# A linear-attention and ReLU-gate block: key weight in five pieces, the query weight loaded late, queries of chunk 1 first, z column three blocks later

## The chip, the cores and the metric

The kernel runs on one core of a Trainium2 chip. The metric is the device time of one execution in microseconds (us); lower is better. Single executions of one kernel scatter here by about 0.3%, so differences of less than 0.7 us are read from the traces, and times are quoted as the median of all runs together with a ratio to the kernel before.

Engines are called as in the profile: PE is TensorE (matmul), DVE is VectorE, ACT is ScalarE, POOL is GpSimd, SP is SyncE, which here only issues DMAs.

## The reference, cut to what matters

```python
# x: 2048 x 640; H = 32 heads of 20; all bf16
xn = layernorm(x)                                   # no scale or bias
q, k, v = split(xn @ wqkv)                          # 3 x (2048 x 640)
phi = lambda t: where(t > 0, t + 1, exp(t)) + 1e-6
kv  = einsum("bhsd,bhse->bhde", phi(k), v)          # per head 20 x 20
z   = einsum("bhsd->bhd", phi(k))                   # sum of the keys over the sequence
o   = (phi(q) @ kv) / (phi(q) . z + 1e-6)
s   = o @ wo
g   = silu(relu(xn @ w1) @ w2)                      # inner size 1728
out = x + s * g
```

## The kernel before: the parts that matter

The 2048 rows are 16 tiles of 128, in 4 chunks of 4 tiles. Chunk 0 is treated apart: its tiles are centred, transposed on PE and multiplied before their variance is known; they are normalised and transposed only later, for the query blocks and the G blocks. From tile 4 on a tile is normalised on DVE (`LN_norm`) and transposed by a DMA (`xnT_dma`), issued by SP. For each chunk PE makes 13 H blocks (`x @ w1`, five matmuls of 512 columns, 1.08 us each), 5 query blocks of the same size, and in between a key product per tile (`K_mm`, ten matmuls of 320 columns, 1.36 us). Later come the G blocks (products of xn and phi(k)), then the products with w2 and the output.

The buffers that the argument needs (a psum bank is a buffer into which PE writes its results; a ring slot is one of a few buffers used in turn):

```python
def K_exp(t, b): ...   # ACT: exp of psum banks b, b+1 into ek[t % 4, 0]
def K_relu(t, b): ...  # ACT: relu of the same banks into ek[t % 4, 1]
def K_fin(t): ...      # DVE, two operations: pk[t] = min(exp, 1) + 1e-6 + relu, reads ek[t % 4]
                       #   so K_exp(4) must wait until K_fin(0) has read slot 0
# key products of tiles 4 and up all use psum banks 0 and 1,
#   so K_mm(5) must wait until K_exp(4) and K_relu(4) have read them
def LN_stats(t): ...   # DVE: two bn_stats, one bn_aggr; then POOL: 1 / sqrt(var + eps)
def LN_norm(t):
    ...                # DVE: xn[t] = (x[t] - mean) * rstd, waits for POOL
    if t + XR < T:
        x_load(t + XR) # SP: next x tile into the slot just read
def z_add(): ...       # POOL: zacc += pk[t], once for each of the 16 tiles
def z_split(): ...     # POOL: zacc as two bf16 parts
def z_col(): ...       # PE: turns these into a column, then DVE builds zmat
```

Load order at the start (SP issues in this order), and the loop over chunks, cut:

```python
x_load(0); x_load(1)
w_load(wqk[:, 0:KA, D:2 * D], ..., ("wk", 0))     # key weight, 2 of 5 row blocks
x_load(2)
w_load(wqk[:, KA:C, D:2 * D], ..., ("wk", 1))     # the other 3
x_load(3)
w1_load(0, "SP"); w1_load(1, "SP")
for t in range(4, XR):
    x_load(t)
...
    w1_load(2, "ACT")                             # 1040 KB, issued by ACT
    ...
    w_load(wqk[:, :, 0:D], A_wqkv[:, 0:D], ("wq",), E="ACT")   # 800 KB, right after it
...
qs = [[], [(0, f) ...] + [(1, f) ...], [(2, f) ...], [(3, f) ...]]   # query blocks by chunk of PE's order
...
            if j == 0:                            # chunk 0, after H block n
                if n in lnat[j]:                  # n = 0..3: tile 4..7
                    LN_stats(t)
                    if n >= 2:
                        K_fin(2 * n - 4); K_fin(2 * n - 3)     # beside the wait for POOL
                    LN_norm(t)
                    xnT_dma(t)
...
                if n == 6:                        # chunk 3
                    z_col()
```

## Time and profile before

| | before |
|---|---|
| median of 4 runs | 227.93 us (227.15 to 227.96) |
| profiled execution | 226.59 us, span of the core 224.9 us |
| PE busy | 215.8 us, 96% of the span |
| waits of PE that a schedule could remove | 4.2 us |

Whether PE is the limit is seen on the page of before, in the busy times and in the clock by slices of the span.

```profile
span 224.9 us, 3501 instructions
...
PE 215.8 (96%) x1432; PEld 132.9 (59%) x1442; DVE 114.9 (51%) x212; ACT 87.1 (39%) x143; POOL 46.7 (21%) x69
...
PEclk9999999999999999999999999999999999999999
```

PE is busy almost always, at the full clock. So the time can fall only where PE stands still. The waits of PE in before say where: engine, buffer and line that waited, what it waited for, then us in total, number of waits, longest.

```profile
PE psT L650 <- POOL regE L645: 1.4, 1, 1.4
PE psT L486 <- DMA reg<-reg: 1.2, 1, 1.2
PE psT L380 <- DVE zero L370: 1.0, 1, 1.0
PE psT L539 <- DMA reg<-reg: 0.6, 1, 0.6
PE psT L486 <- DVE mv L413: 0.4, 1, 0.4
PE psT L486 <- DMA reg<-in_A_wqkv_dram: 0.3, 1, 0.3
```

(The last two lines of that answer, 0.2 us each, are cut.) L650 is the z column, L486 the key products, L539 the query blocks; "reg<-reg" is a transposing DMA. The line L380 is the start of the program. The same waits stand in the timeline of PE of before (start in us, length in us, line, shapes, count, and in brackets the idle time ahead and its end):

```profile
13.03 6.42 PE L561 MATMUL psT<-regX,reg 128*128 128x512 bf16 x29
20.65 1.53 PE L486 MATMUL psT<-reg 128*128 128x320 bf16 x10 [1.20 <-DMA reg<-reg]
...
24.18 1.52 PE L486 MATMUL psT<-reg 128*128 128x320 bf16 x10
...
37.66 1.25 PE L539 MATMUL psT<-reg 128*128 128x512 bf16 x5 [0.61 <-DMA reg<-reg]
...
98.62 0.40 PE L650 MATMUL psT<-ones,regE 128*128 128x1 bf16 x10 [1.36 <-POOL regE L645]
...
114.33 21.90 PE L776 MATMUL psT<-reg 128*128 128x320 bf16 x160
```

13.03 is the first group of H blocks (one of 30 records is missing, so it really began near 12.8). 20.65 is the key product of tile 4, 24.18 that of tile 5, 37.66 the first query block, 98.62 the z column, 114.33 the G blocks. The end of a matmul is modelled. Blocks of five matmuls of 512 columns follow each other every 1.08 us, 0.216 us for each, but a block is shown as 1.24 us long. So an idle time in brackets is about 0.16 us too short.

On DVE, the timeline of before shows tile 4 normalised at 15.04, tile 5 at 17.52, and the first operation of K_fin(0) at 18.92, ahead of the normalisation of tile 6:

```profile
15.04 0.45 DVE L428 TENSOR_SCALAR reg<-reg,mv,rsy 128x640 bf16<-128x640 bf16 x1 [0.99 <-POOL rsy L417]
...
17.52 0.45 DVE L428 TENSOR_SCALAR reg<-reg,mv,rsy 128x640 bf16<-128x640 bf16 x1 [0.99 <-POOL rsy L417]
...
18.92 0.27 DVE L519 TENSOR_SCALAR regE<-regE 128x640 bf16<-128x640 bf16 x1
```

### The profile page before, as it was taken

How to read it: one execution, taken by the hardware profiler on the slowest of the kernel's cores; microseconds unless marked ns; L12 is line 12 of the kernel's file. 1: busy time of each engine (PE TensorE's matmuls, PEld its weight loads, DVE VectorE, ACT ScalarE, POOL GpSimd, SP SyncE). 2: the span in 40 equal slices, each digit the busy share in tenths (PEclk: the TensorE clock that was granted, in tenths of full speed). 3: DMA queues.
4: the chain of work that ended last, by engine and by line, in shares of the span. 5: the costliest groups of instructions: out<-in, count | busy, mean ns of one | idle time of the engine just before them, and what ended most of it. 6: DMA issues, size and time to landing. Idle time of an engine off the chain costs nothing.

```text
span 224.9 us, 3501 instructions
## 1 busy us (share of the span) xinstructions
PE 215.8 (96%) x1432; PEld 132.9 (59%) x1442; DVE 114.9 (51%) x212; ACT 87.1 (39%) x143; POOL 46.7 (21%) x69
## 2 busy tenths in 40 slices
PE   7897998999999999979999999999999999999994
PEld 7553553555544555434467777677767776777672
DVE  4578973797669999764700001940423330413233
ACT  4694765656665576535432113142021102110211
POOL 2243911111006699950000005000000000000000
PEclk9999999999999999999999999999999999999999
DMA  6999456521001233000079969900010100001011
GB/s 184 341 342 195 102 143 111 160 49 29 3 0 31 58 98 109 0 0 0 3 175 272 389 226 372 366 14 3 29 58 32 58 29 32 29 29 58 3 58 60
DMA packets 27712, 23.91 MB, mean 106 GB/s; under 512 B 11824, under 2 KB 27056, under 8 KB 27696
## 3 DMA queue, kind: packets, MB, share of 16 engines
q1 hardware_dynamic: 24464, 19.50, 30.4%
q10 hardware_dynamic: 3232, 4.18, 5.3%
q8 instruction: 11, 0.18, 0.3%
q14 instruction: 5, 0.04, 0.1%
HBM read 15.81 MB, written 5.24 MB: 94 GB/s over the span
## 4 chain that ended last, share of the span: by engine, by line
PE 68%; DVE 12%; POOL 10%; DMA 3%; SPq 2%; issue 2%; ACT 2%; POOLq 0%; DVEq 0%
PE psT L828 25%; PE psT L776 10%; PE psT L561 10%; PE psT L867 9%; POOL zacc L497 8%; PE psT L539 6%; DVE stats L409 3%; DVE reg L428 3%; PE psT L486 3%; DMA reg<-in_A_x_dram 2%; SPq L477 2%; DVE regE L519 1%; PE psT L805 1%; DMA reg<-reg 1%; PE psT L846 1%
## 5 line engine op out<-in xcount | busy, mean ns | idle before, releaser
L828 PE MATMUL psT<-reg,hT 128*128 128x320 bf16 x416 | 60.5, 299 | 0.0
L828 PEld LDWEIGHTS psT<-reg,hT 128*128 128x128 bf16 x416 | 40.3, 98 | 16.5 <-issue 1.1
L561 PE MATMUL psT<-reg 128*128 128x512 bf16 x191 | 45.5, 379 | 0.3 <-issue 0.2
L881 DVE TENSOR_TENSOR reg<-psT,reg 128x640 bf16<-128x640 f32 (+1 forms) x17 | 13.3, 785 | 48.8 <-PE psT L867 47.6
L565 ACT ACTIVATE hT<-psT 128x512 bf16<-128x512 f32 x52 | 30.8, 603 | 18.3 <-PE psT L561 18.3
L561 PEld LDWEIGHTS psT<-reg 128*128 128x128 bf16 x195 | 19.0, 98 | 22.2 <-issue 0.4
L856 ACT ACTIVATE reg<-psT 128x640 bf16<-128x640 f32 x12 | 8.2, 702 | 43.1 <-PE psT L828 23.6
L539 PE MATMUL psT<-reg 128*128 128x512 bf16 x96 | 24.0, 379 | 0.8 <-DMA reg<-reg 0.6
L867 PE MATMUL psT<-reg,pqT 128*128 128x320 bf16 x160 | 24.3, 299 | 0.0
L497 POOL TENSOR_TENSOR zacc<-zacc,reg 128x640 f32<-128x640 f32 x16 | 23.9, 1496 | 1.1
L776 PE MATMUL psT<-reg 128*128 128x320 bf16 x160 | 21.9, 299 | 0.0
L503 ACT ACTIVATE regE<-psT 128x640 bf16<-128x640 f32 x24 | 15.6, 701 | 10.5 <-PE psT L486 9.7
L486 PE MATMUL psT<-reg 128*128 128x320 bf16 x120 | 18.3, 299 | 1.2 <-DMA reg<-reg 1.2
L776 PEld LDWEIGHTS psT<-reg 128*128 128x128 bf16 x160 | 15.7, 98 | 6.2
L867 PEld LDWEIGHTS psT<-reg,pqT 128*128 128x128 bf16 x160 | 15.7, 98 | 6.1
L547 DVE TENSOR_SCALAR regE<-psT 128x512 bf16<-128x512 f32 x20 | 13.7, 683 | 9.3 <-ACT regE L546 9.3
L549 DVE SCALAR_TENSOR_TENSOR pqT<-regE 128x512 bf16<-128x512 bf16 x20 | 17.4, 868 | 0.7
L539 PEld LDWEIGHTS psT<-reg 128*128 128x128 bf16 x100 | 9.6, 98 | 12.1 <-DMA reg<-reg 1.1
L486 PEld LDWEIGHTS psT<-reg 128*128 128x128 bf16 x120 | 11.7, 98 | 7.9 <-DMA reg<-reg 1.9
L546 ACT ACTIVATE regE<-psT 128x512 bf16<-128x512 f32 x20 | 12.0, 598 | 10.9 <-PE psT L539 10.9
L794 DVE TENSOR_TENSOR reg<-psT,mv 128x120 bf16<-128x120 f32 (+1 forms) x6 | 1.1, 260 | 27.6 <-POOL reg L898 27.6
L409 DVE BATCH_NORM_STATS2 stats<-reg 128x6 f32<-128x320 bf16 x32 | 14.1, 477 | 2.1 <-DMA reg<-in_A_x_dram 2.1
(68 smaller groups left out, 167.8 us busy)
## 6 DMA issues: line engine op xcount, KB each, us to landing
reg<-in_A_x_dram SPq DMA_DIRECT2D x16, 160.0 KB, 2.9
scr<-regE SPq DMA_DIRECT2D x4, 640.0 KB, 11.1
reg<-in_A_x_dram SPq DMA_DIRECT2D x4, 640.0 KB, 8.4
out_dram<-reg SPq DMA_DIRECT2D x15, 160.0 KB, 1.8
regE<-scr SPq DMA_DIRECT2D x4, 512.0 KB, 5.0
reg<-in_B_w_dram ACTq DMA_DIRECT2D x1, 1120.0 KB, 12.2
reg<-in_B_w_dram ACTq DMA_DIRECT2D x1, 1040.0 KB, 6.4
reg<-in_A_wo_dram SPq DMA_DIRECT2D x6, 160.0 KB, 3.6
```

The lines of the kernel that those rows point to most:

```text
L409: sc.op("DVE", lambda eng: eng.bn_stats(stats[:, t, a, :], xv[:, HN * a:HN * (a + 1)]), R=[("xin", t % XR)], W=[("stats", t, a)])
L486: fns.append(lambda eng, a=a, k=k, lhs=lhs: eng.matmul(ps[b + a][:, 0:HN], lhsT=lhs[:, k, tok(t)], rhs=wqk[:, k, D + HN * a:D + HN * (a + 1)],
L497: sc.op("POOL", lambda eng: eng.tensor_tensor(out=zacc[:, :], in0=zacc[:, :], in1=pk[:, t, :], op=ALU.add), R=[("zacc",), ("pk", t)], W=[( ...
L503: sc.op("ACT", lambda eng: eng.activation(out=o_.rearrange("p (a n) -> p a n", a=2), in_=ps2(b, HN), func=func, scale=scale), R=[("ps", b) ...
L539: sc.group("PE", [(lambda eng, k=k: eng.matmul(ps[b], lhsT=wqk[:, k, P * f:P * (f + 1)], rhs=xnT[:, k, schunk(j)], start=(k == 0), stop=(k ...
L547: sc.op("DVE", lambda eng: eng.tensor_scalar(out=r_, in0=ps[b], scalar1=0.0, scalar2=1e-6, op0=ALU.max, op1=ALU.add), R=[("ps", b), ("er_e ...
L549: sc.op("DVE", lambda eng: eng.scalar_tensor_tensor(out=pqT[:, f, schunk(j)], in0=e_, scalar=1.0, in1=r_, op0=ALU.min, op1=ALU.add), R=[(" ...
L561: a = sc.group("PE", [(lambda eng, k=k: eng.matmul(ps[b], lhsT=w1_sb[:, k, P * f:P * (f + 1)], rhs=src[:, k, :], start=(k == 0), stop=(k = ...
L565: sc.op("ACT", lambda eng: eng.activation(out=hT[:, f, schunk(j)], in_=ps[b], func=ACTF.Relu), R=[("ps", b)], W=[("hT", j, f)])
L776: fns.append(lambda eng, t=t, a=a: eng.matmul(ps[b + a][:, 0:HN], lhsT=xn[:, t, P * k:P * (k + 1)], rhs=pk[:, t, HN * a:HN * (a + 1)], sta ...
L828: sc.group("PE", [(lambda eng, f=f: eng.matmul(ps[b][:, 0:HN], lhsT=hT[:, f, tok(t)], rhs=w2_sb[:, f, HN * n:HN * (n + 1)], start=(f == 0 ...
L867: sc.group("PE", [(lambda eng, c=c, a=a: eng.matmul(ps[b + a][:, 0:HN], lhsT=pqT[:, c, tok(t)], rhs=wf[:, c, HN * a:HN * (a + 1)], start=( ...
```

## The change

Its intent is to remove four kinds of waits: those among the first key products, at tile 4's key product, at the first query block and at the z column. The key weight comes in five pieces, so that the first key products start on what has landed. Tile 4's statistics move up, and wq, which shares the DMA engines with tile 4's transposing DMA, is issued much later. In chunk 1 the queries of chunk 1 come first, since their transposed tiles are ready by then. The z column moves from after block 6 to after block 9 of chunk 3.

```diff
+    def wk_load(k):
+        dma("SP", ... wqk[:, k, D:2 * D] <- A_wqkv[P * k:P * (k + 1), D:2 * D] ..., W=[("wk", k)])
     x_load(0)
     x_load(1)
-    w_load(wqk[:, 0:KA, D:2 * D], A_wqkv[0:KA * P, D:2 * D], ("wk", 0))
+    wk_load(0)
+    wk_load(1)
     x_load(2)
-    w_load(wqk[:, KA:C, D:2 * D], A_wqkv[KA * P:D, D:2 * D], ("wk", 1))
+    for k in range(KA, C):
+        wk_load(k)
     x_load(3)
     w1_load(0, "SP")
+    x_load(4)
+    x_load(5)
     w1_load(1, "SP")
-    for t in range(4, XR):
-        x_load(t)
+    x_load(6)
+    x_load(7)
@@ prologue; other reorderings of tiles 2 and 3 cut @@
+    for k in range(KA, C):
+        K_mm(0, 2, k, k + 1)
+        K_mm(1, 4, k, k + 1)
...
-    w_load(wqk[:, :, 0:D], A_wqkv[:, 0:D], ("wq",), E="ACT")
+    LN_stats(4)
     bn(3, 0)
@@ loop @@
-    qs = [[], [(0, f) ...] + [(1, f) ...], ...]
+    qs = [[], [(1, f) ...] + [(0, f) ...], ...]
...
-            if ql and (j > 1 or f > 1):
+            if ql:
...
-                if j == 0:
-                    if n >= 2:
-                        K_fin(2 * n - 4)
-                        K_fin(2 * n - 3)
-                    LN_norm(t)
-                    xnT_dma(t)
+            if j == 0:
+                if n < 4:
+                    LN_norm(n + 4)          # now also issues xnT_dma, ahead of the next x load
+                    if n < 3:
+                        LN_stats(n + 5)
+                if n in (3, 4):
+                    K_fin(2 * n - 6)
+                    K_fin(2 * n - 5)
...
+                if n == 8:
+                    w_load(wqk[:, :, 0:D], A_wqkv[:, 0:D], ("wq",), E="ACT")
...
-                if n == 6:
+                if n == 9:
                     z_col()
```

The K_fins of tiles 0 and 1 stood beside the normalisations of tiles 6 and 7. They now follow all four normalisations.

More of the change, by code (lines that the diff above doesn't have):

```diff
@@ L355, in w1_load @@
         w_load(w1_sb[:, :, FC[i]:FC[i + 1]], B_w1[:, FC[i]:FC[i + 1]], ("w1", i), E=E)
+    def wk_load(k):
+        dma("SP", lambda eng: eng.dma_start(wqk[:, k, D:2 * D], A_wqkv[P * k:P * (k + 1), D:2 * D]), W=[("wk", k)])
     x_load(0)
     x_load(1)
-    w_load(wqk[:, 0:KA, D:2 * D], A_wqkv[0:KA * P, D:2 * D], ("wk", 0))
+    wk_load(0)
+    wk_load(1)
     x_load(2)
-    w_load(wqk[:, KA:C, D:2 * D], A_wqkv[KA * P:D, D:2 * D], ("wk", 1))
+    for k in range(KA, C):
+        wk_load(k)
     x_load(3)
     w1_load(0, "SP")
+    x_load(4)
+    x_load(5)
     w1_load(1, "SP")
-    for t in range(4, XR):
-        x_load(t)
+    x_load(6)
+    x_load(7)
     sc.op("DVE", lambda eng: eng.memset(zero[:, :], 0.0), W=[("zero",)])
@@ L430, in LN_norm @@
             op0=ALU.subtract, op1=ALU.mult), R=[("xin", t % XR), ("mv", t), ("rsy", t)], W=[("xn", t)])
+        if t >= 4:
+            xnT_dma(t)
         if t + XR < T:
@@ L489, in K_mm @@
         Rx = [("xnT", t)] if t >= 4 else ([("xcT", t, 0)] if k0 < TS else []) + ([("xcT", t, 1)] if k1 > TS else [])
-        Rw = ([("wk", 0)] if k0 < KA else []) + ([("wk", 1)] if k1 > KA else [])
+        Rw = [("wk", k) for k in range(k0, k1)]
         sc.group("PE", fns, R=Rx + Rw, W=[("ps", b + a) for a in halves])
@@ L598, in bass_recurrent_scan__linear_attn_block__dense_activation_relu__prompt_kernel @@
     bn(0, 1)
-    mean_act(2, 0)
     K_mm(0, 2, 0, KA)
@@ L602, in bass_recurrent_scan__linear_attn_block__dense_activation_relu__prompt_kernel @@
     xcT_copy(1, 6, 1, "ACT")
+    mean_act(2, 0)
     K_mm(1, 4, 0, KA)
     xcT_copy(0, 0, 1, "DVE")
+    aggr(0)
+    bn(1, 0)
+    for k in range(KA, C):
+        K_mm(0, 2, k, k + 1)
+        K_mm(1, 4, k, k + 1)
+    bn(1, 1)
     centre(2)
-    K_mm(0, 2, KA, C)
-    aggr(0)
+    aggr(1)
     transposes(2, 0)
-    xcT_copy(2, 0, 1, "ACT")
-    bn(1, 0)
+    mean_act(3, 0)
+    bn(2, 0)
     xcT_copy(2, 0, 0, "DVE")
-    mean_act(3, 0)
-    K_mm(1, 4, KA, C)
-    bn(1, 1)
-    aggr(1)
+    xcT_copy(2, 0, 1, "DVE")
+    K_exp(0, 2)
+    K_mm(2, 6, 0, KA)
+    K_mm(2, 6, KA, C, (0,))
     centre(3)
-    K_exp(0, 2)
-    K_mm(2, 6, 0, C, (0,))
     transposes(3, 0)
+    K_mm(2, 6, KA, C, (1,))
+    bn(2, 1)
     xcT_copy(3, 0, 0, "DVE")
     xcT_copy(3, 0, 1, "ACT")
-    K_mm(2, 6, 0, C, (1,))
     w1_load(2, "ACT")
     K_relu(0, 2)
-    bn(2, 0)
-    bn(2, 1)
     aggr(2)
@@ L699, in bass_recurrent_scan__linear_attn_block__dense_activation_relu__prompt_kernel @@
     ]
-    qs = [[], [(0, f) for f in range(C)] + [(1, f) for f in range(C)], [(2, f) for f in range(C)], [(3, f) for f in range(C)]]
+    qs = [[], [(1, f) for f in range(C)] + [(0, f) for f in range(C)], [(2, f) for f in range(C)], [(3, f) for f in range(C)]]
     for j in range(1, J):
@@ L704, in bass_recurrent_scan__linear_attn_block__dense_activation_relu__prompt_kernel @@
             plans[j].append(("h", j, f))
-            if ql and (j > 1 or f > 1):
+            if ql:
                 plans[j].append(("q",) + ql.pop(0))
     kat = [{5: 4, 7: 5, 9: 6, 11: 7}, {6: 8, 11: 9, 15: 10, 19: 11}, {6: 12, 9: 13, 12: 14, 15: 15}, {}]
-    lnat = [{0: 4, 1: 5, 2: 6, 3: 7}, {0: 8, 3: 9, 6: 10, 9: 11}, {0: 12, 2: 13, 4: 14, 6: 15}, {}]
+    lnat = [{}, {0: 8, 3: 9, 6: 10, 9: 11}, {0: 12, 2: 13, 4: 14, 6: 15}, {}]
     zfrom = [9, 99, 10, 0]
@@ L715, in bass_recurrent_scan__linear_attn_block__dense_activation_relu__prompt_kernel @@
                 lastW1 = H_block(item[1], item[2])
-            if n in lnat[j]:
-                t = lnat[j][n]
-                LN_stats(t)
-                if j == 0:
-                    if n >= 2:
-                        K_fin(2 * n - 4)
-                        K_fin(2 * n - 3)
-                    LN_norm(t)
-                    xnT_dma(t)
-            if j == 0 and 4 <= n < 8:
-                LN_norm(n - 4)
-            if j == 0 and 8 <= n < 12:
-                xnT_dma(n - 8)
+            if j > 0 and n in lnat[j]:
+                LN_stats(lnat[j][n])
+            if j == 0:
[6 more added lines that the diff above has]
+                    K_fin(2 * n - 5)
+                if 4 <= n < 8:
+                    LN_norm(n - 4)
+                if 8 <= n < 12:
+                    xnT_dma(n - 8)
+                if n == 8:
+                    w_load(wqk[:, :, 0:D], A_wqkv[:, 0:D], ("wq",), E="ACT")
             if j > 0 and n - 1 in lnat[j]:
-                t = lnat[j][n - 1]
-                LN_norm(t)
-                xnT_dma(t)
+                LN_norm(lnat[j][n - 1])
             if n in kat[j]:
```

## The prediction

> **What bounds it now.** TensorE. The page gives PE 215.8 us busy of a 224.9 us span at full clock. The waits of PE name what can be won: 1.36 us before the z column (POOL's split), 1.20 us before the key product of tile 4 (its transposing DMA), 0.61 us before the first query block (another), and 0.34 + 0.45 + 0.21 us among the first key products. Sum 4.2 us; no matmul is removed, so above 2% is nearly out of reach.
>
> **Step by step (timeline durations).**
> 1. Key weight in five pieces, products of tiles 0 and 1 interleaved. Before, six products wait until 7.43 us. Bytes keep their order, so the last piece lands at the same 7.4 us, but the first pieces are used meanwhile: tiles 0 and 1 finish near 8.5 us. Little is left to hide tile 2's transposes (0.3 us plus a 0.3 us copy), so two gaps of 0.3 to 0.4 us appear. H blocks of chunk 0 start at 12.4 us, not 12.8: gain 0.4.
> 2. Tile 4. Its statistics move ahead of tile 3's, so it is normalised near 13.0 us (15.04 before), transposed from 13.5. The transfer took 4.7 us beside the 1040 KB w1 part and 800 KB wq, against 2.7 for quiet ones. The Trainium skill (DMA: Bandwidth & Descriptors, Issuing engines are not separate DMA queues) says that queues share the same 16 engines; 4.7 against 2.7 agrees. With wq gone it should land by 18, before the slot at 18.9: the 1.20 us go.
> 3. Given back. K_fin(0) now follows all four normalisations. Each link of that chain takes 2.48 us (15.04 to 17.52), so K_fin(0) ends near 21.7. The exponential of tile 4 reuses its slot, ScalarE stalls 1.4 us, and tile 5's key product waits 0.65 us for its banks. POOL's z adds (1.5 us each) then overlap the K_fins; DVE operations beside them take about 1.5 us instead of 0.3 to 0.5 (L428 from 23.27), as the Trainium skill (SBUF — State Buffer, SBUF: two separate sides) has it of the shared port pair. So tiles 0 to 3 are normalised later, near 32 us.
> 4. Queries of chunk 1 first: the 0.61 us wait goes. wq, issued near 26 us, lands near 31, needed near 33.5. But tile 8's transposing DMA queues on SP behind those of tiles 0 to 3 (1.28 us each) and is needed as early in chunk 1 as before: a new wait of 0 to 1 us, 0.45 in the middle.
> 5. z column three blocks (3.24 us) later: POOL's split keeps its distance from chunk 2, so the 1.36 us wait goes, with over 1.5 us to spare.
>
> **Sum.** 0.4 + 1.2 + 0.6 + 1.36 - 0.65 - 0.45 = 2.5 us. From 227.93: 225.4 us, 224.0 to 227.0 in 8 of 10 cases. Faster by over 2%: 0.04; within 2%: 0.95; slower: 0.01.
>
> **What would show it.** Waits of PE: none for POOL's split, none of the first query block, none at tile 4's key product; under 1 us at tile 5's, with ScalarE waiting for K_fin(0); at tile 8's perhaps one for a transposing DMA. Timeline: H blocks from 12.4 us; tile 4 normalised near 13.0. Matmul count unchanged.
>
> **What would make it wrong.** x of tile 4 landing after 11 us (late chain, larger waits at tiles 5 and 4); wq landing after 33.5 us; DVE so delayed by z adds that tile 8 comes 2 us late, which eats most of the gain; or none of the new waits, giving 224.

## The result, and the profile after

| | before | changed |
|---|---|---|
| median | 227.93 us (4 runs, 227.15 to 227.96) | 225.05 us (4 runs, 224.81 to 225.6) |
| ratio to before | 1 | 0.9885, 95% interval 0.9857 to 0.9913 |
| span of the profiled execution | 224.9 us | 223.4 us |

A ratio is the mean time of one kernel's fast runs over that of the other's of the same rounds, so it is not quite the ratio of the medians. The change is 1.1% faster, which is within 2%. A second measurement of it (below) gave 0.9901.

The page of the changed kernel, and the waits of its PE:

```profile
span 223.4 us, 3512 instructions
...
PE 216.8 (97%) x1442; PEld 133.8 (60%) x1442; DVE 115.0 (51%) x213; ACT 86.6 (39%) x142; POOL 45.9 (21%) x69
```

```profile
PE psT L495 <- ACT regE L512: 1.6, 1, 1.6
PE psT L387 <- DVE zero L377: 1.1, 1, 1.1
PE psT L495 <- DVE regX L480: 0.2, 1, 0.2
PE psT L495 <- ACT regX L482: 0.2, 1, 0.2
```

Three of the four kinds of waits are gone: no z column, no query block, no transposing DMA. Of the fourth kind, among the first key products, 0.34 + 0.45 + 0.21 us have become 0.22 + 0.17 us; in a second trace of each kernel (e1 and e9 below) it was 0.47 + 0.21 us before and 0.32 + 0.22 + 0.67 + 0.18 us changed, so a gain there is not shown. Line numbers have moved (L495 is a key product, L512 is K_exp and K_relu). A new wait of 1.6 us has come, of a key product for ACT. (PE's 1432 records before and 1442 after are missing records, not less work: its weight loads are 1442 in both.) The timeline of PE of the changed kernel shows which key product it is:

```profile
12.75 6.64 PE L570 MATMUL psT<-regX,reg 128*128 128x512 bf16 x30
19.22 1.52 PE L495 MATMUL psT<-reg 128*128 128x320 bf16 x10
20.58 2.32 PE L570 MATMUL psT<-regX,reg 128*128 128x512 bf16 x10
24.48 1.53 PE L495 MATMUL psT<-reg 128*128 128x320 bf16 x10 [1.58 <-ACT regE L512]
...
99.86 0.39 PE L661 MATMUL psT<-ones,regE 128*128 128x1 bf16 x10
...
112.33 22.15 PE L788 MATMUL psT<-reg 128*128 128x320 bf16 x160
```

Tile 4's key product comes at 19.22 instead of 20.65, a gain of 1.43 us. But tile 5's comes at 24.48 instead of 24.18: all of it has been lost again, and 0.3 us more. The two H blocks from 20.58 on end at 20.58 + 10 x 0.216 = 22.74, so the wait costs 1.74 us from start to start. What ACT did then is the first line of its own waits in the first 40 us of the changed kernel:

```profile
ACT regE L512 <- DVE reg L530: 3.1, 1, 3.1
```

L530 is the second operation of K_fin. And this is DVE's timeline in the changed kernel:

```profile
12.24 0.89 DVE L416 BATCH_NORM_STATS2 stats<-reg 128x6 f32<-128x320 bf16 x2 [1.17 <-DMA reg<-in_A_x_dram]
...
14.37 0.45 DVE L435 TENSOR_SCALAR reg<-reg,mv,rsy 128x640 bf16<-128x640 bf16 x1
...
21.82 0.45 DVE L435 TENSOR_SCALAR reg<-reg,mv,rsy 128x640 bf16<-128x640 bf16 x1 [1.00 <-POOL rsy L424]
...
22.54 0.49 DVE L530 TENSOR_TENSOR reg<-regE 128x640 bf16<-128x640 bf16 x1
...
23.30 1.57 DVE L530 TENSOR_TENSOR reg<-regE 128x640 bf16<-128x640 bf16 x1
```

The statistics of tile 4 wait 1.17 us for its x, to 12.24. Tile 4 is normalised at 14.37 and tile 7 at 21.82, 7.45 us later (three links of 2.48). Only then comes K_fin(0), which ends at 22.54 + 0.49 = 23.03. ACT's exponential of tile 4 follows, then PE's key product of tile 5. (The K_fin at 23.30 takes 1.57 us instead of 0.49; a z add of POOL, from 23.11 to 24.52, runs beside it.)

The whole difference at the G blocks can now be added up from start to start. Waits of before: 1.37 + 0.77 + 1.52 = 3.66 us. New wait: 1.74. Start of the H blocks: 0.06 earlier. 3.66 - 1.74 + 0.06 = 1.98 us; measured 114.33 - 112.33 = 2.00 us.

### The profile page after: what moved, and what is told of

It is laid out like the page before. It is cut to its first block, busy times and chain, and to the rows that moved or that the text cites. A ratio compares the mean times of both kernels' runs of the same rounds, so it can differ in the third digit from the quotient of the medians.

```text
span 223.4 us, 3512 instructions
## 1 busy us (share of the span) xinstructions
PE 216.8 (97%) x1442; PEld 133.8 (60%) x1442; DVE 115.0 (51%) x213; ACT 86.6 (39%) x142; POOL 45.9 (21%) x69
## 3 DMA queue, kind: packets, MB, share of 16 engines
q10 hardware_dynamic: 3232, 4.18, 5.4%
## 4 chain that ended last, share of the span: by engine, by line
PE 83%; DVE 4%; ACTq 3%; DMA 3%; SPq 2%; ACT 1%; POOL 1%; issue 1%; DVEq 0%
PE psT L840 25%; PE psT L570 21%; PE psT L548 10%; PE psT L879 9%; PE psT L495 7%; PE psT L788 6%; DMA reg<-in_A_x_dram 3%; ACTq L780 3%; DVE stats L416 2%; PE psT L817 1%; PE psT L858 1%; PE psT L587 1%; SPq L358 1%; ACTq L776 1%; POOL rsy L424 1%
## 5 line engine op out<-in xcount | busy, mean ns | idle before, releaser
L570 PE MATMUL psT<-reg 128*128 128x512 bf16 x195 | 46.0, 379 | 0.0
L893 DVE TENSOR_TENSOR reg<-psT,reg 128x640 bf16<-128x640 f32 (+1 forms) x17 | 13.3, 785 | 48.8 <-PE psT L879 47.6
L548 PE MATMUL psT<-reg 128*128 128x512 bf16 x100 | 24.8, 379 | 0.0
L879 PE MATMUL psT<-reg,pqT 128*128 128x320 bf16 x160 | 24.3, 299 | 0.0
L512 ACT ACTIVATE regE<-psT 128x640 bf16<-128x640 f32 x24 | 15.6, 701 | 11.4 <-PE psT L495 8.3
L495 PE MATMUL psT<-reg 128*128 128x320 bf16 x120 | 18.3, 299 | 1.6 <-ACT regE L512 1.6
L495 PEld LDWEIGHTS psT<-reg 128*128 128x128 bf16 x120 | 11.7, 98 | 8.3 <-ACT regE L512 2.1
L530 DVE TENSOR_TENSOR reg<-regE 128x640 bf16<-128x640 bf16 x16 | 14.5, 909 | 1.4 <-ACT regE L512 1.0
```

Source lines behind the costliest of these rows:

```text
L495: fns.append(lambda eng, a=a, k=k, lhs=lhs: eng.matmul(ps[b + a][:, 0:HN], lhsT=lhs[:, k, tok(t)], rhs=wqk[:, k, D + HN * a:D + HN * (a + 1)],
L512: sc.op("ACT", lambda eng: eng.activation(out=o_.rearrange("p (a n) -> p a n", a=2), in_=ps2(b, HN), func=func, scale=scale), R=[("ps", b) ...
L530: sc.op("DVE", lambda eng: eng.tensor_tensor(out=pk[:, t, :], in0=e_, in1=r_, op=ALU.add), R=[("ek_e", es), ("ek_r", es)], W=[("pk", t)])
L548: sc.group("PE", [(lambda eng, k=k: eng.matmul(ps[b], lhsT=wqk[:, k, P * f:P * (f + 1)], rhs=xnT[:, k, schunk(j)], start=(k == 0), stop=(k ...
L570: a = sc.group("PE", [(lambda eng, k=k: eng.matmul(ps[b], lhsT=w1_sb[:, k, P * f:P * (f + 1)], rhs=src[:, k, :], start=(k == 0), stop=(k = ...
L879: sc.group("PE", [(lambda eng, c=c, a=a: eng.matmul(ps[b + a][:, 0:HN], lhsT=pqT[:, c, tok(t)], rhs=wf[:, c, HN * a:HN * (a + 1)], start=( ...
```

## The experiments

Theory: up to tile 5's key product the change wins nothing, since this product is tied to K_fin(0), and all the gain comes from the query order and the z column. Rival: each part brings the wait that it removes.

One pair of numbers from each trace placed most effects: the start of tile 5's key product, and the distance from there to the G blocks. All times are in us; the ratio is to before.

| run | tile 4's key product | tile 5's key product | G blocks | tile 5 to G | median | ratio, 95% interval |
|---|---|---|---|---|---|---|
| before | 20.65 | 24.18 | 114.33 | 90.15 | 227.93 | 1 |
| e1, before again | 21.09 | 24.61 | 114.84 | 90.23 | 227.80 | 1.0019 (0.9995 to 1.0043) |
| changed | 19.22 | 24.48 | 112.33 | 87.85 | 225.05 | 0.9885 (0.9857 to 0.9913) |
| e9, changed again | 19.97 | 24.26 | 112.10 | 87.84 | 225.07 | 0.9901 (0.9882 to 0.9920) |
| e2, z column back | 19.80 | 24.61 | 113.98 | 89.37 | 227.03 | 0.9983 (0.9962 to 1.0005) |
| e4, before + two parts | 21.48 | 25.01 | 112.85 | 87.84 | 225.15 | 0.9898 (0.9878 to 0.9919) |
| e3, K_fin early | 20.20 | 23.73 | 111.56 | 87.83 | 223.56 | 0.9837 (0.9810 to 0.9863) |
| e6, weight in two | 20.00 | 23.95 | 111.80 | 87.85 | 224.87 | 0.9904 (0.9866 to 0.9941) |
| e5, x of tile 4 early | 19.55 | 23.49 | 111.33 | 87.84 | 224.21 | 0.9860 (0.9837 to 0.9883) |
| e7, wq early | 21.66 | 25.19 | 113.03 | 87.84 | 225.59 | 0.9921 (0.9898 to 0.9944) |
| e10, K_fin early, wq early | 20.55 | 24.08 | 111.91 | 87.83 | 224.84 | 0.9905 (0.9876 to 0.9933) |
| e8, queries back | 19.71 | 24.42 | 119.01 | 94.59 | 231.16 | 1.0172 (1.0141 to 1.0204) |
| e11, K_fin early, weight in two | 19.43 | 22.94 | 110.78 | 87.84 | 223.72 | 0.9839 (0.9817 to 0.9860) |
| e12, combined | 19.31 | 22.83 | 110.67 | 87.84 | 223.26 | 0.9822 (0.9802 to 0.9842) |

The column "tile 5 to G" takes four values to within 0.08 us: 90.2 for before, 87.84 with both later parts, 89.37 without the z column's move, 94.59 without the query order. Nothing else in this list touches it. What this pair does not see is the stretch from the start of the G blocks to the end of the span: it lasted 110.6 us in before and in e4, 111.1 us in the changed kernel, and up to 112.0 us in e5. Part of this is a wait of PE for ACT in the G blocks (see e12). So a difference of about 1 us between two spans can come from there.

### Noise: both kernels again (e1, e9)

No edit.

> The kernel before, unchanged, against itself: ratio 1.000 within 0.3%, to learn the noise. The profiled execution of before was the fastest (226.59 us against 227.15 to 227.96). If its waits differ from run to run, this second trace shows which: the waits of PE for the transposing DMA of tile 4 (1.20 us), for the first query block (0.61) and for POOL's split (1.36) should all be there again, each within 0.3 us.

Measured: 227.80 us, ratio 1.0019. The three waits were there again, 1.2, 0.7 and 1.4 us. The first microseconds differ from execution to execution: the H blocks began about 0.5 us later than in the first trace, because the second key weight load took 5.1 us to land instead of 4.6, and everything after is shifted by that. After the G blocks began, PE also had a wait of 0.34 us that the first trace had not (it is taken up in e12). So the profiled execution of before was a lucky one, and single spans must not be compared below 1 us.

> The changed kernel, unchanged: ratio to before 0.9885 within 0.3%, tile 5's key product at 24.5 us within 0.2 wherever the H blocks of chunk 0 start (12.7 to 13.5 us), PE's wait there being shorter when they start later.

Measured: 225.07 us, 0.9901. The H blocks began about 0.75 us later than in the first trace, but tile 5's key product started at 24.26, a little earlier (expected 24.3 to 24.7); PE's wait there shrank from 1.58 to 0.60 us. So this start does not follow the H blocks. It follows DVE, which normalised tile 4 at 14.16 here against 14.37.

### The z column back at its old place (e2)

```diff
-                if n == 9:
+                if n == 6:
                     z_col()
```

> The changed kernel with the z column at its old place (after block 6). Theory: POOL's split ends at 98.1 us in the changed kernel whatever PE does, PE would reach the old place near 96.7 us, so a wait of about 1.4 us comes back and the time rises by 1.4 us over the changed kernel. Rival (the z adds of POOL start earlier in the changed kernel, so the place no longer matters): no wait, same time.

Measured: 227.03 us, ratio 0.9983. The distance from tile 5 to the G blocks grew by 1.53 us, and the wait for POOL's split came back, as the first line of the waits of PE of this run shows:

```profile
PE psT L661 <- POOL regE L656: 1.4, 1, 1.4
```

The theory holds. The z column is the largest single part of the gain. The times differ by more (225.05 against 227.03), but the intervals of the ratios allow anything from 1 to 3 us.

### Before with the query order and the z column alone (e4)

```diff
-    qs = [[], [(0, f) ...] + [(1, f) ...], ...]
+    qs = [[], [(1, f) ...] + [(0, f) ...], ...]
...
-                if n == 6:
+                if n == 9:
                     z_col()
```

> The kernel before with only two parts of the change: queries of chunk 1 ahead of those of chunk 0, and the z column moved back. Theory (what the key weight pieces, the late wq and the early tile 4 win before 20.6 us is all lost at tile 5's key product, 24.48 us against 24.18 before): this is as fast as the changed kernel or 0.3 us faster, so 2 to 2.5 us faster than before. Rival (every part brings its own wait): slower than the changed kernel by 1.2 to 1.6 us.

Measured: 225.15 us, ratio 0.9898, against 0.9885 and 0.9901 for the changed kernel. Two lines of the diff give the whole gain. Tile 4's product still waits 1.4 us for its transposing DMA, and the key weight cost waits of 1.0 and 0.5 us in this execution, but the distance from tile 5 to G is that of the changed kernel to 0.01 us. The rival (1.2 to 1.6 us slower) is out.

### K_fin in the gaps of the normalisation chain (e3)

```diff
                     if n < 3:
                         LN_stats(n + 5)
-                if n in (3, 4):
-                    K_fin(2 * n - 6)
-                    K_fin(2 * n - 5)
+                    K_fin(n)
```

> The changed kernel with K_fin(0..3) put one each into the gaps in which DVE waits for POOL between the normalisations of tiles 4 to 7. Theory (the wait of PE before tile 5's key product, 1.6 to 1.75 us, comes from ScalarE waiting 3.1 us for K_fin(0)): both waits go, tile 5's key product starts at about 22.8 us instead of 24.48, and the time falls by about 1.5 us against the changed kernel. Rival (PE would wait there anyway, for the transposing DMA of tile 5 or for a busy ScalarE): start at 24.0 or later, same time within 0.4 us.

Measured: 223.56 us, ratio 0.9837; 1.1 to 1.5 us faster than the changed kernel, by the two ratios of that. ACT's wait for K_fin(0) and PE's at tile 5 are both gone. The second operation of K_fin(0) on DVE, and tile 5's key product, which no wait precedes:

```profile
16.33 0.49 DVE L530 TENSOR_TENSOR reg<-regE 128x640 bf16<-128x640 bf16 x1
...
23.73 1.52 PE L495 MATMUL psT<-reg 128*128 128x320 bf16 x10
```
Tile 5's product started at 23.73, not at the expected 22.8: in this execution the H blocks began about 0.6 us later (PE waited 0.8 us for tile 3's centring, behind a late x load) and tile 4's product waited 0.22 us for its DMA. The normalisation chain itself became only slightly longer, a link of 2.66 us against 2.48, since the K_fins fill DVE's waits for POOL. The cause of the new wait is shown: it was where K_fin(0) stood.

### The key weight in two pieces (e6)

```diff
-    wk_load(0)
-    wk_load(1)
+    dma("SP", ... wqk[:, 0:KA, D:2 * D] in one ..., W=[("wk", k) for k in range(KA)])
     x_load(2)
-    for k in range(KA, C):
-        wk_load(k)
+    dma("SP", ... wqk[:, KA:C, D:2 * D] in one ..., W=[("wk", k) for k in range(KA, C)])
```

> The changed kernel with the key weight in two pieces again, as before, all else as changed. Theory (gains ahead of tile 5's key product are absorbed there): the H blocks of chunk 0 start 0.1 to 0.5 us later than with five pieces, but tile 5's key product starts at 24.5 us within 0.2, and the time stays at a ratio of 0.988 to the kernel before, within 0.25%. Rival (each wait removed counts): tile 5's key product and the end move by the same 0.1 to 0.5 us as the H blocks.

Measured: 224.87 us, ratio 0.9904, with a wide interval. The time is as expected; the reason was not. Tile 5's product started at 23.95, not 24.5, with only 0.27 us of wait. The theory had taken K_fin(0) as fixed. In fact the three extra issues of the five pieces hold up SP by about 0.46 us each. With two pieces x of tile 4 was issued at 4.18 us instead of 5.51, and landed at 10.6 us instead of 12.2 (12.0 in e9): the same bytes in the same order. Tile 4 was normalised at 13.85 instead of 14.37 (14.16 in e9). So the five pieces pushed back the very load on which the new critical chain hangs. How much this load costs varies: DVE waited 1.17 us for it in the first trace of the changed kernel, but 0.21 us in e9, where DVE itself was busy until 11.8. The next run moves the load.

### x of tile 4 ahead of the first w1 part (e5)

```diff
+    x_load(4)
     w1_load(0, "SP")
-    x_load(4)
     x_load(5)
```

> The changed kernel with the load of x of tile 4 issued ahead of the first w1 part. Theory (the late K_fin(0) is late because DVE waits 1.17 us, to 12.24 us, for x of tile 4, which was issued 1.3 us later because of the three extra weight pieces): tile 4 is normalised at 13.0 to 13.4 us instead of 14.37, ScalarE's wait for K_fin(0) shrinks by 1 us, tile 5's key product starts at 23.2 to 23.7 us, and the time falls by about 1 us against the changed kernel. Rival (the chain is bound by POOL and DVE, not by the load): start at 24.3 or later, same time.

Measured: 224.21 us, ratio 0.9860 against 0.9901 for the changed kernel on the same chip, so about 0.9 us. The timeline lines of DVE and of PE:

```profile
13.39 0.45 DVE L435 TENSOR_SCALAR reg<-reg,mv,rsy 128x640 bf16<-128x640 bf16 x1
...
23.49 1.53 PE L495 MATMUL psT<-reg 128*128 128x320 bf16 x10 [0.26 <-ACT regE L512]
```

Tile 4 is normalised 1 us earlier and tile 5's product starts 1 us earlier than in the first trace of the changed kernel. The chain is: issue of x of tile 4, its landing, four normalisations, K_fin(0), K_exp(4), K_mm(5). Both ends of it have now been moved, and PE moved with each. From the normalisation of tile 4 to tile 5's product it was 10.10 or 10.11 us in all six traces with the late K_fin(0) and the late wq (changed, e2, e5, e6, e8 and e9), wherever the H blocks began. In e5 DVE no longer waited for x at all; its own earlier work ended just before 11.32, when the statistics of tile 4 began.

### wq early again (e7, e10)

e7 is the changed kernel with this; e10 is e3 with this.

```diff
+    w_load(wqk[:, :, 0:D], A_wqkv[:, 0:D], ("wq",), E="ACT")
     LN_stats(4)
...
-                if n == 8:
-                    w_load(wqk[:, :, 0:D], A_wqkv[:, 0:D], ("wq",), E="ACT")
```

> The changed kernel with wq issued early again. Theory: tile 4's transposing DMA lands in more than 4 us instead of about 3, so PE waits 0.3 to 1 us before tile 4's key product, but tile 5's still starts at 24.5 us within 0.2 and the time is that of the changed kernel. Rival (the late wq is what removed the 1.2 us wait and so is worth it): the time rises by 0.5 to 1.2 us.

Measured: 225.59 us, ratio 0.9921. PE waited 2.5 us at tile 4's product, far more than expected:

```profile
21.66 1.53 PE L495 MATMUL psT<-reg 128*128 128x320 bf16 x10 [2.50 <-DMA reg<-reg]
```

This exceeded what tile 5 could hide: ACT was not waited for at all, and tile 5's product came at 25.19, 0.7 us later than in the changed kernel. The theory's number is wrong here, and the rival's (0.5 to 1.2 us) is right in size, though most of the 2.5 us were hidden. The transposing DMA, issued at 14.55, took 7.1 us. What the queues moved between 15 and 17 us (queue, packets, MB, share of the time of 16 engines) explains it; q10 is ACT's queue with the w1 part and wq, q1 is SP's with the transposing DMA. First e7, then the changed kernel:

```profile
q10 hardware_dynamic: 541, 0.75, 101.4%
```

```profile
q1 hardware_dynamic: 484, 0.12, 52.5%
q10 hardware_dynamic: 213, 0.33, 44.7%
```

In e7 SP's queue did not move one packet in these 2 us. wq was issued at 11.14 and landed after 10.0 us, at 21.1; the transposed tile came at 21.66. In before wq landed at 11.42 + 8.0 = 19.4 and the tile at 20.6. With wq in flight, issuing the transposing DMA 1.3 us earlier did not make it land earlier. So the early tile 4 is of no use without the late wq; the late wq alone was not run.

> The version with K_fin in the gaps (which was 1.1 us faster than the changed kernel) and wq issued early again. Now nothing after tile 4's key product hides a delay: theory says that the wait there, 0.22 us with the late wq, grows to 0.7 to 1.5 us, and the time by as much (0.5 to 1.3 us). Rival (the late wq is worth nothing anywhere): the wait stays below 0.4 us and the time within 0.3 us.

Measured: 224.84 us, ratio 0.9905. The wait at tile 4's product grew from 0.22 to 0.78 us. Tile 5's product came 0.35 us later than in e3, in an execution whose H blocks began 0.2 us earlier, so the trace gives 0.55 us, at the low end of what was expected. The two ratios differ by 0.7%, or 1.5 us, but they come from different chips and each has an interval of 0.6%. The theory is supported, and its size is not settled to better than 1 us.

### The queries of chunk 0 first again (e8)

```diff
-    qs = [[], [(1, f) ...] + [(0, f) ...], ...]
+    qs = [[], [(0, f) ...] + [(1, f) ...], ...]
```

> The changed kernel with the queries of chunk 0 ahead of those of chunk 1 again. In the changed kernel the transposing DMAs of tiles 0 to 3 are issued from 32.4 us on, one each 1.28 us, so the last lands near 39 us. Theory: PE waits about 3.9 us at the first query block (reached at 35.04 us), and the time rises by about 3.5 to 3.9 us over the changed kernel, to that of before or a little above. Rival (only the 0.6 to 0.8 us of before come back): 0.8 us.

Measured: 231.16 us, ratio 1.0172: 6.1 us slower than the changed kernel, where 3.5 to 3.9 were expected. The wait itself was exactly as expected. The rest is the clock. The timeline of PE around the wait:

```profile
33.90 1.24 PE L570 MATMUL psT<-reg 128*128 128x512 bf16 x5
39.02 2.31 PE L548 MATMUL psT<-reg 128*128 128x512 bf16 x5 [3.88 <-DMA reg<-reg]
41.13 2.34 PE L570 MATMUL psT<-reg 128*128 128x512 bf16 x5
43.26 1.86 PE L548 MATMUL psT<-reg 128*128 128x512 bf16 x5
44.96 1.24 PE L570 MATMUL psT<-reg 128*128 128x512 bf16 x5
```

And the same stretch in windows of this run (the PE clock stands behind the busy times, 1.00 is full speed):

```profile
30.00:35.00 5.00, 5.00 (x28) 2.50 (x26) 4.20 (x12) 3.68 (x7) 0.21 (x1) 1.00 0.89 245
39.00:44.00 5.00, 4.98 (x12) 1.79 (x13) 1.74 (x3) 1.09 (x2) 0.00 (x0) 0.50 0.01 3
46.00:51.00 5.00, 5.00 (x28) 2.64 (x27) 3.90 (x9) 3.04 (x6) 0.79 (x2) 1.00 0.53 166
```

After the idle time PE ran at half its clock. The 15 matmuls from 39.02 to 44.96 took 5.94 us instead of 15 x 0.216 = 3.24, which is 2.70 us lost on top. 3.88 + 0.16 (the modelled end) + 2.70 = 6.74; the distance from tile 5 to G grew by 94.59 - 87.84 = 6.75. The Trainium skill (TensorE: Matmul & The Clock Gate, What's actually happening) says that an idle window of about 3.4 us drops the clock from 2.4 to 1.2 GHz, and that about as long a busy one restores it. This trace agrees: 3.88 us of idleness, a clock of 0.50, and full speed again about 5 us later, which is longer than the stated 3.4 us. The next longest wait, 2.5 us in e7, was too short: the clock after it was 1.00.

The query order is thus not only a gain of 0.77 us. After the other edits it is needed: the four normalisations of tiles 0 to 3 end later (near 31.9 us), and their transposing DMAs are issued from 32.4 us on.

### Towards a faster version (e11, e12)

e11 is e3 with the key weight in two pieces as in e6.

> The version with K_fin in the gaps, and the key weight in two pieces. Nothing hides the start of the H blocks any more. Theory (five pieces win at most 0.2 us at the key products, and their three extra issues of 0.46 us each delay x of tile 4): no wait at tile 4's key product, tile 5's starts within 0.3 us of the five-piece version's 23.73 us, and the time is the same within 0.3%. Rival (five pieces are worth 0.4 us or more): 0.4 us slower or more.

Measured: 223.72 us, ratio 0.9839 (e3: 0.9837). No wait at tiles 4 and 5; tile 5's product at 22.94, even 0.8 us earlier than in e3, where 0.3 us at most were expected. So nothing shows a gain from the five pieces here. But the start of the H blocks varies by up to 0.7 us between executions and each ratio by about 0.5 us, so the rival's 0.4 us is not excluded.

e12 joins e3 and e5, and moves two small loads. In several traces (e1, e3, e5, e6, e9) PE waited 0.3 to 0.7 us in the G blocks for ACT, which was still held by the issue of these loads: 5.7 us for two DMAs in the changed kernel, from 114.76 us on.

```diff
     # e3's and e5's edits, and:
-    for u in range(2):
-        dma("ACT", ... w2l[64 * u:64 * (u + 1), :] ..., W=[("w2l", u)], extra=[lastW1])
     for k in range(C):
         lastG = G_block(k, (0, 2, 0, 2, 4)[k])
+        if k == 2:
+            for u in range(2):
+                dma("ACT", ... w2l[64 * u:64 * (u + 1), :] ..., W=[("w2l", u)], extra=[lastW1])
```

> A version meant to be the fastest: K_fin in the gaps, x of tile 4 issued ahead of the first w1 part, and the two small w2 loads issued by ScalarE after the third G block instead of before the first (their issue held ScalarE for 5.7 us and PE waited up to 0.4 us for its copy). Theory: no wait of PE at tiles 4 and 5, none in the G blocks; 0.3 to 0.8 us faster than the version with K_fin in the gaps alone, so a ratio to before of about 0.981. Rival (no gain left there): 0.984.

Measured: 223.26 us (223.11 to 223.55), ratio 0.9822. It is the fastest kernel by its median, with the narrowest scatter; the intervals of e3, e11 and e12 overlap, so 0.3 us between them is not proven by the times, and neither the theory (0.981) nor the rival (0.984) is excluded. The waits of its PE are all that is left:

```profile
PE psT L387 <- DVE zero L377: 1.1, 1, 1.1
PE psT L495 <- DVE regX L480: 0.2, 1, 0.2
PE psT L495 <- ACT regX L482: 0.2, 1, 0.2
PE psT L570 <- issue: 0.2, 1, 0.2
```

Apart from the start, 0.6 us of waiting remain. That moving the two loads helped is not shown: eight traces with the loads at their old place, the changed kernel's first among them, had no wait of PE for ACT in the G blocks either. All twelve runs gave correct results.

## Why the prediction was right, point by point

The time was predicted at 225.4 us and came out at 225.05, inside the range of 224.0 to 227.0, and "within 2%" was given 0.95. The gain of 2.5 us compares with 2.0 us at the G blocks in the first pair of traces, 2.7 us in the second (e1 and e9), and 2.6 us (1.15%) by the ratio. The structure was right: the waits at tile 4, the first query block and the z column go, and part of the gain is given back at tile 5. That the total came so close is in part luck, as the last point shows. The terms of the sum were off in both directions.

| step | predicted | measured |
|---|---|---|
| 1. key weight in five pieces | H blocks 0.4 us earlier, at 12.4 | 12.75, 0.06 earlier; in the repeats (13.3 before, 13.5 changed) no gain |
| 2. tile 4's wait | gone, 1.2 us | gone, 1.37 us from start to start |
| 2. tile 4 normalised | 13.0 | 14.37 |
| 3. new wait at tile 5 | 0.65 us, ACT held 1.4 us, K_fin(0) ends 21.7 | 1.74 us, ACT held 3.1 us, K_fin(0) ends 23.03 |
| 3. tiles 0 to 3 normalised | near 32 us | 31.9 |
| 4. first query block | 0.6 us gained | 0.77 gained |
| 4. new wait at tile 8 | 0.45 us, 0 to 1 | none |
| 5. z column | 1.36 us gained | 1.52 gained |

- The term that was mis-sized most is step 3, "tile 5's key product waits 0.65 us for its banks": it cost 1.74 us. Its mechanism (K_fin(0) behind all four normalisations, then slot 0, ACT and the two banks) was right, and e3 proved it by removing it. The size failed because tile 4 was normalised at 14.37 instead of 13.0. That 13.0 needs x of tile 4 by about 10.9 us (an estimate: 13.0 less the 2.13 us from the statistics to the normalisation in the trace); it was waited for until 12.24. The prediction had named this under what would make it wrong ("x of tile 4 landing after 11 us"), but of the pieces it says only that "Bytes keep their order"; the three extra issues on SP are not in it. e6 shows these as a cause, since with two pieces the load landed at 10.6 us, and e5 shows that the chain follows the load. They are not the whole: even so tile 4 was normalised at 13.85 (e6) and 13.39 (e5), never at 13.0, because DVE was still busy.
- Step 1 won nothing. The last key products of tiles 0 and 1 were done near 8.7 us instead of 8.5, and tile 2's transposes and copies stood bare, as foreseen. The gain of 0.4 us was an estimate below what varies from one execution to the next.
- Step 2 was right that wq must go, for the reason given; e7 shows a stronger effect than expected. But the time did not need it: e4 leaves wq and tile 4 as they were in before, and is as fast as the changed kernel.
- Step 4's new wait at tile 8 did not come. The larger wait at tile 5, which delayed PE, is not the reason: in e12, without that wait, PE reached tile 8 at 39.85 us instead of 41.51 and did not wait either. The DMA did not queue behind those of tiles 0 to 3: SP issued it at 38.75 (37.09 in e12), right after DVE had normalised tile 8 at 38.28 (36.62). DVE does this behind its work on the first query block, so it moves with PE: from this normalisation to tile 8's product it was 3.23 us in both traces.
- The terms of steps 1 to 3 are not three independent gains and losses. They meet at one place: tile 5's product starts when the later of two chains ends, so whatever comes earlier on PE's side only lengthens the wait there. The prediction put this start at 24.18 - 0.4 - 1.2 + 0.65 = 23.23 us; it came at 24.48, which is 1.25 us worse. The wait at tile 8 that did not come (0.45), the query block (0.17 more) and the z column (0.16 more) gave 0.78 us back. So errors of opposite sign cancelled, and 2.5 against 2.0 us at the G blocks is closer than the single terms were.

## What to carry to other kernels

When work is moved ahead on one engine, look for what it was moved past: here a small operation on an engine with half its time free (K_fin on DVE) held a ring slot, and through it ACT, two psum banks and PE. Before adding up removed waits, find the next place where two chains meet, for only the later chain counts there; the start of such a place, and the distance to the next, are two numbers that sort most effects into before and after. And one wait of PE of nearly 4 us (e8) cost 2.7 us more than itself, because the clock fell.

## What the Trainium skill lacked or had wrong

- DMA: Bandwidth & Descriptors (Queues, rings and completion order) says that a DMA engine takes turns between the queues that have work, packet by packet. In e7, with 1.8 MB issued on ACT's queue from 10.62 us on, that queue moved 541 packets between 15 and 17 us and SP's queue none, though SP had been issuing a transposing DMA since 14.55; it landed 7.1 us after its issue, against 3.3 without wq. An even sharing would not give this. It is not peculiar to transposing DMAs: in before, an ordinary x load issued at 15.51 us, ahead of the transposing DMA, landed after 4.3 us, against 2.5 for such a load without wq, and there too SP's queue moved no packet between 15 and 17 us. What held SP's queue back these runs do not tell.
- The same page (Issuing engines are not separate DMA queues) calls the sequencer's issue time usually small beside the DMA, and gives no number there. For one load of 160 KB that agrees: 0.43 to 0.47 us of issue on SP, 2.3 us or more to landing. But issues add up: three more of them delayed x of tile 4 from 4.18 to 5.51 us, and tile 5's product came 0.3 to 0.5 us later than in e6. And an issue can take much longer: right behind the two large w2 loads, that of two small loads held ACT for 5.7 us; 9 us later in the program, in e12, it took 1.16 us.
- Nothing was wrong in SBUF — State Buffer (SBUF: two separate sides), which says that VectorE and GpSimd share a pair of ports that one of them holds for a whole instruction while the other is blocked. K_fin's tensor_tensor took 1.57 us beside a z add of POOL and 0.49 us without.
- TensorE: Matmul & The Clock Gate (What's actually happening) agrees on the fall of the clock (3.88 us idle, clock 0.50); full speed came back after about 5 us, later than the 3.4 us it gives. Here the wait of 3.88 us cost 2.70 us more in slow matmuls, and the wait of 2.5 us in e7 did not lower the clock.
